# A gated mix of a state-space convolution and a spectral filter on one core: new instruction sequences with 64 fewer spare matmuls, one scale folded into its neighbours, six output rows on two other engines

## The chip, the cores and the metric

The kernel runs as one program on one NeuronCore of a Trainium2 chip. The metric is the device time of an execution in microseconds (us). The names of the engines in the profile: PE is TensorE (matmuls; PEld is its weight load), DVE is VectorE, ACT is ScalarE, POOL is GpSimd, and SP is SyncE, which here only starts DMA transfers.

## What is computed

The output is a mix of two branches over an input of 2048 positions by 640 channels. Branch a convolves each channel with a kernel K that is made from the parameters; branch b is a two-dimensional real Fourier transform, a product with complex weights, and the inverse. The gate g is one number for each position.

```python
def _A_ref(u, log_A_real, A_imag, C_real, C_imag, log_dt, D_skip):
    dt = jnp.exp(log_dt)
    A = -jnp.exp(log_A_real) + 1j * A_imag
    C = (C_real + 1j * C_imag) * dt[:, None]
    P = jnp.exp((A * dt[:, None])[:, :, None] * pos[None, None, :])
    K = 2.0 * jnp.einsum("dn,dnl->dl", C, P).real
    Kf, Uf = jnp.fft.rfft(K, L2), jnp.fft.rfft(u_t, L2)
    y = jnp.fft.irfft(Uf * Kf[None, :, :], L2)[:, :, :L]
    return y + u * D_skip[None, None, :]
def _B_ref(x, w_r, w_i):
    X = jnp.fft.rfft2(x, axes=axes) * (w_r + 1j * w_i)
    return jnp.fft.irfft2(X, s=(S, D), axes=axes)
x = A_u
g = _sigmoid((x * gate_w).sum(-1, keepdims=True))
return g * a + (1 - g) * b
```

## The kernel before

All Fourier transforms are matmuls with tables of cosines and sines, in two steps (64 by 64 positions). The program has five stages, which overlap at their edges.

Stage A (`phase_a`, first half) transforms the input: `stage1w` (L532) and `stage2` (L546) are PE matmuls, ACT (later DVE too) copies each result out of PSUM (L579), and SP writes it to the DRAM buffer `u_d` (L626). At the same time `phase_p` works out the parameters from C, A and dt on DVE, with a few ACT functions: magnitude and angle of C (an arctangent at L489, finished by L490 to L498) and a logarithm (L511). They are split into bfloat16 parts and sent through DRAM.

Stage F (second half of `phase_a`) is branch b in nine blocks: transposes (L700), products along the channels (L710), the filter on DVE (L728 to L746), and the way back (L764, then L771 and L773 on DVE).

Stage B (`phase_b`) makes K in 40 steps. For each step PE multiplies the parameters with a table of positions; ACT then takes exponentials for the magnitudes (`mags`, L832 on PE, L833 on ACT) and sines for the phases (`outer` and `inner`, L840 on PE, L846 and L852 on ACT); DVE (L860 to L862) and POOL (L865, L866) multiply magnitude and phase; PE sums over the states (`kgen`, L876), and ACT copies the sums out (L882). Stages F and B share the time between about 80 and 380 us: their instructions are interleaved on every engine. The exponential and the sine lie in different function tables of ACT, so that each change from one to the other loads a table (ACT_TABLE_LOAD).

Stages C and D transform K, multiply it with the transformed input in `fronts` (L971 to L974), transform back in `backs` (L988, L990, written to DRAM at L997 and L1000), and make the output rows in `last_e` (L1030, L1037) and `last_c` (L1030, then L1048 for the last quarter of the channels, L1050 and L1051 for the others). The output of the last quarter is written in three chunks of 6, 6 and 4 rows of 160 numbers for each partition; a row is one instruction of L1048.

Nothing is scheduled at run time. The functions only record their operations in a list; the table `ORDER` is a permutation of that list, and `Program.write` issues the operations in that order. Each engine runs its own operations strictly in that order, and an operation waits until what it reads is written and the buffer that it writes is free. Two kinds of operations do no part of the computation, and `ORDER` places them as well. `SPARE` gives a number of matmuls of a constant with itself (L406), 128 by 128, whose result nobody reads; there are 278. `PRIME` gives a number of one-element ACT functions (L409), placed ahead of the first use of another function table, so that the load happens there; there are 23 for the exponential, 23 for the sine, and one each for arctangent, logarithm and sigmoid.

Of the kernel before, what the change touches and what calls it, by code (L numbers as in the profile page):

```python
# [412 lines left out]
def phase_p(tc, A, T):  # L413
# [3 lines left out]
    with ExitStack() as ctx:  # L417
# [72 lines left out]
        V.tensor_scalar(out=ph[:, :, :], in0=ph[:, :, :], scalar1=1.0 / (2 * math.pi), scalar2=None, op0=ALU.mult)  # L490
        V.tensor_scalar(out=y[:, :, :], in0=ph[:, :, :], scalar1=-2.0, scalar2=0.25, op0=ALU.mult, op1=ALU.add)
        V.tensor_tensor(out=y[:, :, :], in0=y[:, :, :], in1=ab[:, :, :], op=ALU.mult)
        V.tensor_tensor(out=ph[:, :, :], in0=ph[:, :, :], in1=y[:, :, :], op=ALU.add)
# [449 lines left out]
def phase_d(tc, A, T, ctx, out):  # L943
# [95 lines left out]
    def last_c(c, a, n):  # L1039

        oe = oes.pop((c, a))
        p = last("p_c", lambda g: T.e3[c < 3], lambda g, r: t3s[c][r, 4 * a + n * g:4 * a + n * g + n], n)
        ot = o2.tile([128, 2, 3, 160], F32, tag="ot", name="ot")
        if c == 3:
            for j in range(2):
                for i in range(n):
                    x = 8 * j + a + i
                    V.scalar_tensor_tensor(out=ot[:, j, i], in0=p[:, j, i], scalar=T.gate[:, 0, x:x + 1], in1=oe[:, j, i], op0=ALU.mult, op1=ALU.add)  # L1048
        else:
            V.tensor_tensor(out=ot[:, :, 0:n], in0=p, in1=gate(0, a, n), op=ALU.mult)  # L1050
            G.tensor_tensor(out=ot[:, :, 0:n], in0=ot[:, :, 0:n], in1=oe[:, :, 0:n], op=ALU.add)  # L1051
        (G if c < 2 else nc.sync).dma_start(out[c].rearrange("p (j a) d -> p j a d", j=2)[:, :, a:a + n], ot[:, :, 0:n])
# [24 lines left out]
SPARE = (128, 278), (32, 0)  # L1077
PRIME = 23, 23, 1, 1, 1
# [97 lines left out]
```

## Time and profile before

| what | us |
|---|---|
| median of 3 runs | 536.0 |
| the three runs | 535.62, 536.0, 543.41 |
| the profiled execution, whole time | 533.92 |
| its span in the profile | 531.9 |

The profile is one execution of the program. Its page gives the busy time of each engine and groups of instructions by source line; a row of a group reads line, engine, operation, output and inputs, count, then busy us and mean ns, then the idle time of the engine just ahead of these instructions. The share of slices in which the engines are busy shows the stages: ACT and DVE are nearly full in the middle and ACT is nearly idle in stage D, where the DMA engines are full instead.

```profile
PE   8999999899999989999989999998999997999993
DVE  5994236989899999598688696879575673767754
ACT  3787887699989877899969989966433242332210
DMA  8969526782313335132040231413997799799986
```

Each digit is the busy share in a fortieth of the span, in tenths. PE looks full everywhere, but in the middle a part of its work is the spare matmuls.

### The profile page before, as it was taken

Reading aid. Unit: us, or ns where it says so; the run is one execution under the profiler, and the core shown is the slowest. Engines: PE = TensorE matmul, PEld = TensorE weight load, DVE = VectorE, ACT = ScalarE, POOL = GpSimd, SP = SyncE. Lnnn points to the kernel's source line nnn. Section 1 sums busy time; section 2 is a strip of 40 time slices with the busy share of each in tenths; the row PEclk is TensorE's granted clock in tenths of the full one; section 3 lists DMA queues with packets and bytes.
Section 4 is the critical chain, followed back from the end, with each engine's and each line's share of the span. In section 5 each row is a group of like instructions: output and inputs, shape, how many; then the busy total and the mean of one; then the engine's idle time right before and its main releaser. Section 6 shows DMA issues by size and latency. Waiting matters only on the chain. (4 is left out here: it accounts for less than half of the span.)

```text
span 531.9 us, 19458 instructions
## 1 busy us (share of the span) xinstructions
PE 499.3 (94%) x8600; PEld 409.5 (77%) x8600; DVE 397.6 (75%) x548; ACT 354.6 (67%) x505; POOL 226.1 (43%) x236
## 2 busy tenths in 40 slices
PE   8999999899999989999989999998999997999993
PEld 6899797788887878877768888886797886887740
DVE  5994236989899999598688696879575673767754
ACT  3787887699989877899969989966433242332210
POOL 1003213674766253746554525526431245337350
PEclk9999999999999999999989999999999999999998
DMA  8969526782313335132040231413997799799986
GB/s 318 361 199 339 171 81 215 250 256 84 101 67 110 125 103 170 46 118 70 30 147 32 67 110 52 127 55 123 358 338 240 247 374 390 261 321 311 340 266 234
DMA packets 58363, 101.17 MB, mean 190 GB/s; under 512 B 4980, under 2 KB 42136, under 8 KB 58248
## 3 DMA queue, kind: packets, MB, share of 16 engines
q1 hardware_dynamic: 34680, 67.82, 37.2%
q10 hardware_dynamic: 20368, 21.79, 12.3%
q0 software_dynamic: 3232, 10.33, 5.8%
q8 instruction: 67, 1.10, 0.8%
q14 instruction: 16, 0.13, 0.1%
HBM read 60.60 MB, written 39.65 MB: 188 GB/s over the span
## 5 line engine op out<-in xcount | busy, mean ns | idle before, releaser
L546 PE MATMUL psum<-sbuf,sbuf 128*64 128x160 f32 x1056 | 89.2, 308 | 6.5 <-ACT sbuf L536 2.7
L546 PEld LDWEIGHTS psum<-sbuf,sbuf 128*64 128x64 f32 x1056 | 72.7, 134 | 19.3 <-issue 6.5
L406 PE MATMUL psum<-sbuf 128*128 128x128 f32 x556 | 79.0, 287 | 0.0
L532 PE MATMUL psum<-sbuf,sbuf 128*64 128x128 f32 x1280 | 77.2, 274 | 0.2 <-issue 0.2
L406 PEld LDWEIGHTS psum<-sbuf 128*128 128x128 f32 x556 | 67.0, 192 | 11.3 <-issue 9.1
L532 PEld LDWEIGHTS psum<-sbuf,sbuf 128*64 128x64 f32 x1280 | 72.2, 137 | 3.8 <-issue 2.5
L710 PE MATMUL psum<-sbuf 64*128 64x161 f32 (+1 forms) x864 | 68.9, 305 | 4.3 <-DVE sbuf L771 2.2
L710 PEld LDWEIGHTS psum<-sbuf 64*128 64x128 f32 (+1 forms) x864 | 60.8, 182 | 9.4 <-DVE sbuf L771 2.3
L862 DVE TENSOR_TENSOR sbuf<-sbuf,psum 128x1024 f32<-128x1024 f32 x40 | 48.5, 1216 | 25.3 <-ACT psum L852 25.2
L833 ACT ACTIVATE sbuf<-psum 128x1024 f32<-128x1024 f32 (+1 forms) x80 | 60.9, 803 | 4.8 <-PE psum L832 3.1
L409 ACT ACT_TABLE_LOAD x48 | 61.6, 1283 | 0.8
L974 POOL TENSOR_TENSOR sbuf<-sbuf 128x320 f32<-128x320 f32 (+1 forms) x36 | 32.1, 893 | 68.3 <-DVE sbuf L972 57.3
L990 ACT COPY sbuf<-psum 128x640 f32<-128x640 f32 x32 | 21.9, 693 | 52.3 <-PE psum L988 36.1
L865 POOL TENSOR_TENSOR sbuf<-sbuf,sbuf 128x512 f32<-128x512 f32 x24 | 34.0, 1417 | 31.2 <-ACT sbuf L846 22.4
L579 ACT COPY sbuf<-psum 128x512 f32<-128x512 f32 (+2 forms) x58 | 35.3, 626 | 17.1 <-PE psum L532 11.7
L536 ACT COPY sbuf<-psum 128x512 f32<-128x512 f32 x40 | 23.9, 620 | 34.2 <-PE psum L532 22.8
L852 ACT ACTIVATE psum<-psum 128x1024 f32<-128x1024 f32 x40 | 40.3, 1008 | 9.3 <-PE psum L840 9.2
L876 PEld LDWEIGHTS psum<-sbuf 128*32 128x32 f32 x2560 | 37.9, 110 | 9.1 <-issue 7.1
L876 PE MATMUL psum<-sbuf 128*32 128x64 f32 x2560 | 44.4, 221 | 0.5 <-issue 0.4
L988 PEld LDWEIGHTS psum<-sbuf,sbuf 64*128 64x128 f32 x528 | 37.6, 186 | 6.8 <-issue 4.6
L988 PE MATMUL psum<-sbuf,sbuf 64*128 64x160 f32 x528 | 42.7, 305 | 0.1
L846 ACT ACTIVATE sbuf<-psum 128x1024 f32<-128x1024 f32 x40 | 40.7, 1017 | 2.8 <-PE psum L840 2.8
(133 smaller groups left out, 827.9 us busy)
## 6 DMA issues: line engine op xcount, KB each, us to landing
u_d<-sbuf SPq DMA_DIRECT2D x32, 320.0 KB, 4.2
sbuf<-u_d ACTq DMA_DIRECT2D x16, 640.0 KB, 6.7
s_d<-sbuf ACTq DMA_DIRECT2D x24, 320.0 KB, 5.8
sbuf<-s_d SPq DMA_DIRECT2D x6, 960.0 KB, 8.4
sbuf<-in_w_l SPq DMA_DIRECT2D x8, 644.0 KB, 4.1
sbuf<-u_d SPq DMA_DIRECT2D x8, 640.0 KB, 4.8
k_d<-sbuf SPq DMA_DIRECT2D x20, 256.0 KB, 2.3
sbuf<-k_d SPq DMA_DIRECT2D x8, 640.0 KB, 6.9
```

What stands on the lines that cost most here:

```text
L406: nc.tensor.matmul(spare[x:x + cols, i, :], c1[:, x:x + cols], c1[:, 128:256], start=True, stop=True)
L409: nc.scalar.activation(prime[0:1, i:i + 1], c1[0:1, 0:1], f)
L532: nc.tensor.matmul(p[64 * ri:64 * ri + 64, q // 4, 0:512].rearrange("p (h x) -> p h x", h=2)[:, :, 64 * (q % 4):64 * (q % 4) + 64], src[:, ...
L546: nc.tensor.matmul(p[64 * j:64 * j + 64, y, 160 * ro:160 * ro + 160], T.w2[:, x, ro, :], t1[:, x // 2 if x < 32 else K0 // 2, :, x % 2 if ...
L579: return (V.tensor_copy if T.dve and dst.home.name == "ut" else S.copy)(dst, src)
L710: P.matmul(p[:st.nl, c, 161 * i:161 * i + 161], src[r, k, x, 0:st.nl], td[r, w, k, :], start=k == 0, stop=k == 2)
L833: S.activation(ef[:, :, c:c + n], p[:, :, 0:n], AF.Exp)
L846: S.activation(sc.rearrange("p d v i -> p (d v i)"), p.rearrange("p j w -> p (j w)"), AF.Sin, scale=TWO_PI)
L852: S.activation(f, f, AF.Sin, scale=TWO_PI)
L862: V.tensor_tensor(out=x[:, 0].rearrange("p d (h j) -> p d h j", h=2), in0=e[:, :, 0:64].rearrange("p d (h j) -> p d h j", h=2), in1=cx.uns ...
L876: P.matmul(st.pb[32 * r:32 * r + 32, o, :], y[:, ri, 4 * qq + r, :], x[:, ri, 4 * qq + r, :], start=t % 2 + qq + 1 - ri == 0, stop=t % 2 * ...
L988: P.matmul(p[:, j, 160 * i:160 * i + 160], T.w3[r, pr, im, :], t2[r, h + i, im], start=im == 0, stop=im == 1)
```

## The change

Three things change.

First, in `phase_p` the arctangent's factor 1/(2 pi) no longer has an instruction of its own. The line that multiplied `ph` is gone; the next line takes -1/pi in place of -2, and the addition after it becomes a `scalar_tensor_tensor` that multiplies and adds at once.

Second, in `last_c`, for the last quarter of the channels, the first two rows of the second half of each chunk, so six rows of 16, are no longer one DVE instruction each. ACT multiplies the row with the gate out of PSUM, and POOL adds the row of the other branch.

Third, `ORDER` is another permutation, and its fillers change in number: `SPARE` from 278 to 214, `PRIME` from 23 and 23 to 25 and 24.

```diff
         S.activation(ph[:, :, :], q[:, :, :], AF.Arctan)
-        V.tensor_scalar(out=ph[:, :, :], in0=ph[:, :, :], scalar1=1.0 / (2 * math.pi), scalar2=None, op0=ALU.mult)
-        V.tensor_scalar(out=y[:, :, :], in0=ph[:, :, :], scalar1=-2.0, scalar2=0.25, op0=ALU.mult, op1=ALU.add)
+        V.tensor_scalar(out=y[:, :, :], in0=ph[:, :, :], scalar1=-1.0 / math.pi, scalar2=0.25, op0=ALU.mult, op1=ALU.add)
         V.tensor_tensor(out=y[:, :, :], in0=y[:, :, :], in1=ab[:, :, :], op=ALU.mult)
-        V.tensor_tensor(out=ph[:, :, :], in0=ph[:, :, :], in1=y[:, :, :], op=ALU.add)
+        V.scalar_tensor_tensor(out=ph[:, :, :], in0=ph[:, :, :], scalar=1.0 / (2 * math.pi), in1=y[:, :, :], op0=ALU.mult, op1=ALU.add)
...
                     x = 8 * j + a + i
-                    V.scalar_tensor_tensor(out=ot[:, j, i], in0=p[:, j, i], scalar=T.gate[:, 0, x:x + 1], in1=oe[:, j, i], op0=ALU.mult, op1=ALU.add)
+                    if j and i < 2:
+                        S.activation(ot[:, j, i], p[:, j, i], AF.Copy, scale=T.gate[:, 0, x:x + 1])
+                        G.tensor_tensor(out=ot[:, j, i], in0=ot[:, j, i], in1=oe[:, j, i], op=ALU.add)
+                    else:
+                        V.scalar_tensor_tensor(out=ot[:, j, i], in0=p[:, j, i], scalar=T.gate[:, 0, x:x + 1], in1=oe[:, j, i], op0=ALU.mult, op1=ALU.add)
...
-SPARE = (128, 278), (32, 0)
-PRIME = 23, 23, 1, 1, 1
+SPARE = (128, 214), (32, 0)
+PRIME = 25, 24, 1, 1, 1
...
-2 0 2190 2167 3 7 1 2191 4+2 8 6 2192 9 2169 19 2170 2172+3 2168 2184 2175 20+16 2176 12 2177+5 36 2182+2 2185 17 2187 10 2171 38+16 37 11 54 2186 55
...
```

What the new order does is best seen in the rows of an engine. A row names the line, the operation, what it writes and reads (a number at the end is a memory area), its shape, and how many alike follow each other. Line numbers after L490 are lower by one in the changed kernel, and from L1050 on higher by three.

The first place is PE in the middle of the program, ahead of the longest run of spare matmuls. L832 are the matmuls of `mags`, L406 the spare ones, L700 transposes. Before:

```order
L832 LDWEIGHTS sbuf_68
L832 MATMUL psum_77<-sbuf_68 128x256
L406 MATMUL psum_77<-sbuf_67 128x128 x19
L832 LDWEIGHTS sbuf_68
L832 MATMUL psum_77<-sbuf_68 128x512
L832 LDWEIGHTS sbuf_68
L832 MATMUL psum_77<-sbuf_68 128x512
```

And in the changed kernel, at the same `mags`:

```order
L831 LDWEIGHTS sbuf_68
L831 MATMUL psum_77<-sbuf_68 128x256
L406 MATMUL psum_77<-sbuf_67 128x128 x13
L831 LDWEIGHTS sbuf_68
L831 MATMUL psum_77<-sbuf_68 128x512
L831 LDWEIGHTS sbuf_68
L831 MATMUL psum_77<-sbuf_68 128x512
```

The run of 19 has become one of 13; at this point 46 spare matmuls have been issued before and 31 now.

The second place is PE at the forward products (L710) of a later block, which stand at about 250 us in the profile of before. L876 is `kgen`, L700 the transposes. Before:

```order
L406 MATMUL psum_77<-sbuf_67 128x128 x6
L710 MATMUL psum_77<-sbuf_73 128x161 x12
L832 LDWEIGHTS sbuf_68
L832 MATMUL psum_77<-sbuf_68 128x512
L832 LDWEIGHTS sbuf_68
L832 MATMUL psum_77<-sbuf_68 128x512
L406 MATMUL psum_77<-sbuf_67 128x128 x5
L876 MATMUL psum_77<-sbuf_71 32x64 x32
```

And now:

```order
L406 MATMUL psum_77<-sbuf_67 128x128 x2
L709 MATMUL psum_77<-sbuf_73 128x161 x12
L699 MATMUL psum_77<-sbuf_67,sbuf_73 128x64 x16
L406 MATMUL psum_77<-sbuf_67 128x128 x3
L839 LDWEIGHTS sbuf_69
L839 MATMUL psum_77<-sbuf_68,sbuf_69 128x256
```

The transposes, which stood one `kgen` later, have come ahead of it, the pair of `mags` has gone to another place, and 5 spare matmuls stand where 11 stood.

The third place is the end of ACT's program. Before, its last work is the copies and writes of `backs`:

```order
L990 COPY sbuf_69<-psum_77 128x2x2x160
L997 DMA s3f_d<-sbuf_72 32x160
L1000 DMA s3f_d<-sbuf_69 64x4x160 x2
L997 DMA s3f_d<-sbuf_72 32x160
L1172 UNCONDITIONAL_BRANCH
```

And now:

```order
L989 COPY sbuf_69<-psum_77 128x2x2x160
L996 DMA s3f_d<-sbuf_72 32x160
L999 DMA s3f_d<-sbuf_69 64x4x160 x2
L1048 ACTIVATE sbuf_73<-psum_77,sbuf_67 128x160 x6
L1175 UNCONDITIONAL_BRANCH
```

The six rows of `last_c` stand behind everything that ACT did before; POOL's six additions (L1049) likewise come last on POOL.

143 rows, old and new, of the table ORDER are left out of this document.

## The prediction

> **What bounds the kernel now.** I read the page first, then the busy time by stage, then who waits for whom, then the order of time around the spare matmuls, and last the end of the program. The page and the stage in which F and B overlap:
>
> ```profile
> PE 499.3 (94%) x8600; PEld 409.5 (77%) x8600; DVE 397.6 (75%) x548; ACT 354.6 (67%) x505; POOL 226.1 (43%) x236
> L406 PE MATMUL psum<-sbuf 128*128 128x128 f32 x556 | 79.0, 287 | 0.0
> 80.00:380.00 300.00, 286.41 (x5334) 234.65 (x5332) 254.02 (x320) 254.44 (x341) 156.81 (x152) 0.99 0.37 117
> ACT psum L852 <- PE psum L840: 9.2, 8, 3.4
> ACT sbuf L753 <- PE psum L710: 7.3, 9, 1.5
> DVE sbuf L862 <- ACT psum L852: 16.7, 10, 5.6
> PE psum L710 <- DVE sbuf L771: 2.2, 1, 2.2
> ```
>
> The second row is the spares: 278 operations (two passes each, so 556 records) fill 79.0 us of PE. The third row is the stretch from 80 to 380 us: after its length come the busy times of PE, weight load, DVE, ACT and POOL, then the granted clock and the share of the DMA engines. PE is busy for 286.4 of 300 us, but without the 79.0 it has 207 us of real work, and DVE and ACT have 254 each. So in the middle no engine is full with useful work: ACT and DVE each stand idle for about 46 us, waiting in turn for PE and for each other, and PE's own waits are covered by spares. Of PE's uncovered waits the longest is the 2.2 us of the last row.
>
> Are the spares themselves on the path? That shows where a run of them ends:
>
> ```profile
> 119.71 0.50 PE L832 MATMUL psum<-sbuf 48*128 48x512 bf16 x4
> 120.14 4.51 PE L406 MATMUL psum<-sbuf 128*128 128x128 f32 x38
> 122.18 1.28 ACT L409 ACT_TABLE_LOAD   x1
> 123.58 3.05 ACT L833 ACTIVATE sbuf<-psum 128x1024 f32<-128x1024 f32 x4
> 124.63 0.76 PE L832 MATMUL psum<-sbuf 48*128 48x512 bf16 x4
> 125.32 0.94 PE L406 MATMUL psum<-sbuf 128*128 128x128 f32 x6
> ...
> 257.76 2.72 PE L406 MATMUL psum<-sbuf 128*128 128x128 f32 x22
> 259.41 1.00 ACT L846 ACTIVATE sbuf<-psum 128x1024 f32<-128x1024 f32 x1
> 260.46 0.96 PE L840 MATMUL psum<-sbuf,sbuf 64*128 64x256 bf16 x8
> ```
>
> At 120.14 PE begins 19 spares (38 records). The next `mags` matmul needs a PSUM buffer that ACT frees with the first of four exponentials; these start at 123.58 and take 1.00 us for a buffer, so the buffer is free at 124.6, and PE goes on at 124.63. At 257.76 it is the sine of L846, which ends at 260.41, and PE goes on at 260.46. A run of spares thus stands in for a wait of PE on ACT and ends when the wait ends, within 0.1 us here. The middle is bounded by the chain ACT to PE to ACT (and DVE), not by PE.
>
> After 380 us the bound is another:
>
> ```profile
> 380.00:400.00 20.00, 19.41 (x308) 18.65 (x306) 14.41 (x22) 7.40 (x12) 7.97 (x11) 1.00 0.97 364
> 480.00:496.00 16.00, 15.91 (x222) 12.54 (x200) 12.44 (x18) 4.11 (x7) 9.51 (x10) 1.00 1.00 326
> sum 116.00, PE 111.82 PEld 94.08 DVE 76.36 ACT 37.78 POOL 46.13; mean PE 18.64 PEld 15.68 DVE 12.73 ACT 6.30 POOL 7.69
> ...
> 0.00:40.00 40.00, 37.28 (x698) 32.01 (x700) 33.43 (x60) 26.82 (x48) 3.13 (x9) 1.00 0.79 292
> 40.00:80.00 40.00, 38.53 (x642) 34.84 (x641) 14.19 (x26) 31.85 (x52) 10.00 (x17) 1.00 0.57 197
> ```
>
> These are the first and last of six stretches from 380 to 496 us and their sum: PE is full with real work (111.8 of 116 us), and the DMA engines nearly so (0.97 and 1.00 here). The last two rows are stage A, where PE has real work for 75.8 of 80 us.
>
> **The change part by part.**
>
> *Spares.* Two runs of the rows above give the price: 38 records take 4.51 us and 6 take 0.94, so 16 spares more take 3.57 us, 0.223 us each, with 0.27 us for a run whatever its length. In PE's listing of before there are 63 runs with 278 spares: 62.0 + 17.0 = 79.0 us, just the page's row. The new order has 54 runs with 214: 47.7 + 14.6 = 62.3 us. So 16.7 us of filling go, most of it between the places that stood at 110 and 325 us. What is it worth? If the new order has as much less waiting for PE as it has less filling, the middle shrinks by 16.7 us. That is a reading of the order's fillers and not of a measured wait: before, the fillers fit the waits, as shown, and PE's uncovered waits are few; I take it that they fit as well after. Without runs' fixed part it would be 64 x 0.223 = 14.3 us, with the mean of the page's row (79.0 / 278) 18.2 us. If the fillers only went and the waits stayed, it is worth 0. I take 16.7, because the fit of the old fillers is the nearest evidence; both ends stay for the range.
>
> Is there room? In 283.3 us (300 - 16.7) DVE's 254 us would be 90%. ACT gets more work:
>
> *Table loads.* `PRIME` grows by three (two exponentials, one sine), and ACT's listing has three table loads more, all between 80 and 380 us.
>
> ```profile
> L409 ACT ACT_TABLE_LOAD  x48: 1283/1283/1283, 22.4 to 344.6; - x48
> L409 ACT ACTIVATE sbuf<-sbuf x49: 191/202/204, 15.6 to 345.9; 1x1 f32<-1x1 f32 x49
> ```
>
> Three loads with their one-element functions take 3 x 1.485 = 4.5 us, so ACT would have 258.9 us of work in 283.3, 91%, and its idle time would fall from 45.6 to 24.4 us. That fits, but not with much to spare. The loads' price lies inside the middle: 0 if ACT's lost idle time holds it, 4.5 us at most. I take 0, since the new fillers already stand for an order with these loads; a sum that counts them in full is 4.5 us longer.
>
> *The arctangent's scale, the start and stage D.*
>
> ```profile
> L490 DVE TENSOR_SCALAR sbuf<-sbuf x1: 489/489/489, 24.9 to 24.9; 128x640 f32<-128x640 f32 x1
> 11.17 0.33 SPq L605 DMA_DIRECT2D sbuf<-in_t_w  x1
> 12.03 0.33 SPq L586 DMA_DIRECT2D sbuf<-in_u_l  x1
> 26.29 2.93 PE L546 MATMUL psum<-sbuf,sbuf 128*64 128x160 f32 x35
> sbuf<-in_t_w SPq DMA_DIRECT2D x3, 704.0 KB, 9.0
> ```
>
> L490 goes and takes 0.49 us of DVE with it; the addition that now multiplies too stays an instruction of the same size. DVE runs this while PE does stage A's 75.8 us of real work, which covers it: 0, at most -0.5. If that cover were gone, the parameters would be ready 0.5 us sooner. On SP's queue the third part of the table `w2` (L605, at 11.17) moves behind one more load of `u` that waits for PE (at 12.03), so it leaves about a microsecond later, and with 9.0 us to land is there at about 22; the second step, L546, gets to its last third during the 2.93 us from 26.29. Cost 0, or 1 us if the queue is slower. In stage D the order of `last_e` and `last_c` among `backs` changes, but the work is the same and PE's whole idle time there is 116 - 111.8 = 4.2 us: that is the most it could gain, and I take it as the most it could lose; 0 in the sum.
>
> *Six rows on ACT and POOL.* The end of the program:
>
> ```profile
> 524.93 3.08 DVE L1048 SCALAR_TENSOR_TENSOR sbuf<-psum,sbuf,sbuf 128x160 f32<-128x160 f32 x10 [0.69 <-PE psum L1030]
> 525.89 0.77 PE L1030 MATMUL psum<-sbuf,sbuf 64*32 64x320 f32 x16 [0.99 <-issue]
> L992 ACT COPY sbuf<-psum x4: 286/286/287, 418.0 to 504.3; 64x160 f32<-64x160 f32 x4
> L974 POOL TENSOR_TENSOR sbuf<-sbuf x36: 513/876/1115, 382.5 to 507.0; 128x320 f32<-128x320 f32 x32, 64x160 f32<-64x160 f32 x4
> ```
>
> Before, DVE ends its ten rows of the last two chunks at 528.01, and the last transfer follows. After, the last chunk is ready when PE ends at 526.66. ACT's two rows, by the copy of as many elements, take 0.29 each and end at about 526.95 and 527.24. POOL's additions take 0.51 each (its shortest row is of 160 elements), one after the other: 527.5 and 528.0. DVE's two rows end near 527.3. So the last chunk leaves at 528.0 to 528.2 instead of 528.01, with POOL last where DVE was last. The first two chunks leave up to 0.5 us sooner, which the last transfer does not need. Cost 0, from -0.7 (if POOL hands over at once and the transfers no longer queue) to +0.7 (with hand-overs between engines). Nothing queues behind the ACT rows: they are ACT's last.
>
> *What is not in the order: collisions and the clock.*
>
> ```profile
> L688 DVE TENSOR_TENSOR sbuf<-sbuf x18: 541/758/3934, 92.6 to 265.9; 128x384 f32<-128x384 f32 x16, 64x384 f32<-64x384 f32 x2
> 268.70:272.10 3.40, 1.22 (x18) 1.09 (x20) 3.39 (x5) 2.50 (x4) 2.38 (x4) 1.00 0.28 77
> 272.10:275.50 3.40, 3.40 (x28) 2.78 (x25) 2.00 (x2) 0.75 (x1) 0.00 (x0) 0.50 0.87 211
> ```
>
> One L688 instruction, from 265.9, took 3.93 us where its kind takes 0.54 at best; everything on DVE behind it came late, PE waited the 2.2 us shown above, was busy for 1.22 of 3.40 us, and the next 3.4 us ran at clock 0.50. That one event cost about 2.2 + 1.7 = 3.9 us. [...] 0 in the sum.
>
> The sum against the profiled execution: 533.92 - 16.7 = 517.2. The median of the runs stands 536.0 - 533.92 = 2.1 us above it, so I forecast 519.3 us. A measurement of this kernel can tell about 2% from no change, 10.7 us: below 525.3 is faster, above 546.7 slower.
>
> **The rivals.**
>
> *Part of the gain.* ACT becomes the chain: with 258.9 us of work and waits that cannot be covered, the middle gives half, 8.3 us: 536.0 - 8.3 = 527.7. For it: ACT falls from 45.6 us of idle to 24.4, and 4.5 us of loads are new. Against: DVE and ACT still have 9% and more each.
>
> *None.* Fillers were taken out and the waits stayed. Then PE stands idle where it filled, and the time is 536.0, up to 540.5 with the loads. For it: PE waits for ACT, and fewer spares speed up nothing by themselves. Against: the runs of before end with the waits, so their lengths do follow them.
>
> *Slower, by the clock.* It takes no gain at all, and uncovered waits. PE then has 16.7 us more idle time in the same 300. By the two rows above a stretch of 3.4 us with 2.2 us idle halves the clock of the next, which costs 1.7 us of work. 16.7 us are enough for seven such stretches, 7 x 1.7 = 12 us: 548. It decides from the seventh, so all of that idle time would have to come in pieces of 2.2 us. [...]
>
> **How the numbers follow.** The forecast has 0.64 (512 to 525), more gain than that 0.05 (the event of 265.9 gone and stage D better as well), part of the gain 0.12, none 0.13, slower 0.06. The predicted time is the forecast's. The range is 512 to 536: 512 is 519.3 less the 1.5 us between 16.7 and 18.2, the 3.9 of the event and 2 of stage D's 4.2; 536 is no gain. Outside lie the 0.05, the 0.06 and half of "none", 0.18 together. Faster is 0.64 + 0.05 = 0.69, the same 0.12 + 0.13 = 0.25, slower 0.06.
>
> **What would show it.** Right: the stretch up to the last `kgen` is some 17 us shorter, spares have about 62 us of PE, ACT's idle time in the middle is near 24 us, PE's own waits stay as short as they were, and the runs of spares still end with an ACT instruction. Wrong: PE idles in the middle by ten microseconds or more, ACT's idle time stays over 40, the clock shows more than one or two stretches of 0.50. The end is right if the last POOL addition ends some 1.4 us after the last matmul. The forecast fails most simply if the new fillers were not cut to the waits.

## The result, and the profile after

| | before | after |
|---|---|---|
| median of 20 runs each, us | 536.52 (530.67 to 544.8) | 538.41 (534.29 to 541.8) |
| ratio of the times, 95% interval | | 1.006 (1.0038 to 1.0081) |
| span of the profiled execution, us | 531.9 | 536.4 |

The ratio is taken over the executions within 1.5% of the fastest of the same kernel, so it is not the ratio of the two medians, which stand 1.9 us apart. By the ratio the change cost about 3 us (0.6%), where 16.7 us were forecast to be gained. The page of the changed kernel, first the busy times, then the row of the spares, then the granted clock in fortieths of the span:

```profile
PE 489.0 (91%) x8472; PEld 399.9 (75%) x8472; DVE 402.6 (75%) x541; ACT 359.0 (67%) x517; POOL 232.0 (43%) x242
L406 PE MATMUL psum<-sbuf 128*128 128x128 f32 x428 | 62.1, 288 | 0.0
PEclk9999899999999999999999999998999999999996
```

The spares went as counted: 62.1 us of PE instead of 79.0. But PE's share of the span fell with them. Where the time went is seen from the same instructions in both traces. The columns are the ends, in us from the span's start.

| end of | before | after | difference |
|---|---|---|---|
| last matmul of stage A's first half (L532; L531 after) | 77.8 | 86.0 | +8.2 |
| first `kgen` matmul (L876; L875) | 80.8 | 89.4 | +8.6 |
| last `kgen` matmul | 379.7 | 382.5 | +2.8 |
| last `backs` matmul (L988; L987) | 510.9 | 510.8 | -0.1 |
| last matmul (L1030; L1029) | 526.7 | 528.2 | +1.5 |
| span | 531.9 | 536.4 | +4.5 |

So there are three effects: a later start (8.6 us), a middle that is shorter by 5.8 us and not by 17, and an end that is longer by 3 us after the last matmul. Stage D made up 2.9 us in this execution up to its last `backs` matmul, and 1.6 of them were lost again up to the last matmul: 8.6 - 5.8 - 2.9 + 1.6 + 3.0 = 4.5.

*The start.* PE's rows of the changed kernel in order of time, with the start, the length, and in brackets the wait ahead and what ended it:

```profile
55.73 2.78 PE L531 MATMUL psum<-sbuf,sbuf 128*64 128x128 f32 x46
63.16 0.61 PE L831 MATMUL psum<-sbuf 48*128 48x512 bf16 x2 [4.64 <-DMA sbuf<-par_d]
63.70 5.23 PE L531 MATMUL psum<-sbuf,sbuf 128*64 128x128 f32 x48
```

The stretches of 3.4 us around them, with the length, the five busy times and the granted clock:

```profile
58.40:61.81 3.41, 0.12 (x2) 0.00 (x0) 0.00 (x0) 2.07 (x3) 2.75 (x6) 1.00 0.95 288
61.81:65.22 3.41, 2.06 (x16) 1.63 (x18) 0.00 (x0) 1.02 (x1) 0.00 (x0) 0.50 0.35 82
65.22:68.64 3.42, 3.42 (x36) 3.42 (x34) 0.00 (x0) 0.60 (x1) 0.00 (x0) 0.50 0.00 0
```

The first `mags` matmul (L831) now stands ahead of the last 24 matmuls of its block of stage A, and PE waits 4.64 us there for the magnitude parameters. Before, it stood behind them and waited 1.2 us:

```profile
59.27 0.39 PE L832 MATMUL psum<-sbuf 48*128 48x512 bf16 x1
60.84 0.49 PE L832 MATMUL psum<-sbuf 48*128 48x512 bf16 x3 [1.19 <-DMA sbuf<-par_d]
```

On POOL, which issues the loads of the parameters, the issue of the magnitudes waits longer for the write of the same data. The row of before:

```profile
53.88 1.02 POOL L818 DMA_DIRECT2D sbuf<-par_d  x2 [0.48 <-DMA par_d<-sbuf]
```

The row of after:

```profile
56.48 1.03 POOL L817 DMA_DIRECT2D sbuf<-par_d  x2 [2.39 <-DMA par_d<-sbuf]
```

After the wait the clock is 0.50 for 6.8 us: 48 records that take 2.84 us at full clock (a row of another run, at the end of this document) take 5.23.

There is a second, smaller cost ahead of it. The page's rows of the first step of the transform, before and after, end with the idle time of PE ahead of these instructions and what ended it:

```profile
L532 PE MATMUL psum<-sbuf,sbuf 128*64 128x128 f32 x1280 | 77.2, 274 | 0.2 <-issue 0.2
L531 PE MATMUL psum<-sbuf,sbuf 128*64 128x128 f32 x1280 | 81.0, 281 | 1.6 <-DMA sbuf<-in_u_l 1.6
```

With the changed order PE waits 1.6 us, up to 9.4 us from the start of the span, for a part of the input `u`; before it did not. All seven profiled executions with the changed start have this wait (1.6 to 2.7 us).

*The middle*, from the first to the last `kgen` matmul, in before:

```profile
80.80:379.70 298.90, 285.31 (x5322) 233.79 (x5312) 253.51 (x319) 253.46 (x339) 156.81 (x152) 0.99 0.37 117
```

And in after:

```profile
89.40:382.50 293.10, 272.15 (x5182) 220.31 (x5172) 255.90 (x318) 255.90 (x345) 160.53 (x154) 0.99 0.38 120
```

PE is busy for 13.2 us less and the stretch is 5.8 us shorter, so PE's idle time grows from 13.6 to 21.0 us. ACT is idle for 37.2 us instead of 45.4, not for 24.4.

*The end.* The last line of the program, where the engines meet: a row gives line, queue, instruction, count, shortest, median and longest duration in ns, and the first and last start. In before:

```profile
L1172 POOLq DRAIN  x3: 46/102/9637, 512.7 to 531.6; - x3
L1172 SPq DRAIN  x3: 7/7/13, 531.1 to 531.4; - x3
```

And in after:

```profile
L1175 POOLq DRAIN  x3: 46/102/6643, 529.0 to 536.2; - x3
L1175 SPq DRAIN  x3: 7/7/13, 533.0 to 535.9; - x3
```

SP's first DRAIN comes when the last output has landed, at 531.1 before and at 533.0 after: the last write of the output was issued at 528.0 and 529.8 and took 3.0 and 3.1 us to land. POOL's long DRAIN began at 512.7 before and was over at 522.3, long before that; after, it begins at 529.0 (POOL's last addition ends at 529.76) and ends at 535.6, 2.6 us after the last output. In all 18 traces the span ends 0.8 us after the later of the two.

### The profile page after: what moved, and what is told of

Its sections match the earlier page's. It is cut to its first block, busy times and chain, and to the rows that moved or that the text cites. A ratio compares the mean times of both kernels' runs of the same rounds, so it can differ in the third digit from the quotient of the medians.

```text
span 536.4 us, 19217 instructions
## 1 busy us (share of the span) xinstructions
PE 489.0 (91%) x8472; PEld 399.9 (75%) x8472; DVE 402.6 (75%) x541; ACT 359.0 (67%) x517; POOL 232.0 (43%) x242
## 5 line engine op out<-in xcount | busy, mean ns | idle before, releaser
L545 PEld LDWEIGHTS psum<-sbuf,sbuf 128*64 128x64 f32 x1056 | 72.9, 134 | 15.4 <-issue 9.1
L531 PE MATMUL psum<-sbuf,sbuf 128*64 128x128 f32 x1280 | 81.0, 281 | 1.6 <-DMA sbuf<-in_u_l 1.6
L531 PEld LDWEIGHTS psum<-sbuf,sbuf 128*64 128x64 f32 x1280 | 75.7, 141 | 5.1 <-issue 2.4
L832 ACT ACTIVATE sbuf<-psum 128x1024 f32<-128x1024 f32 (+1 forms) x80 | 60.8, 800 | 9.1 <-PE psum L831 7.1
L406 PE MATMUL psum<-sbuf 128*128 128x128 f32 x428 | 62.1, 288 | 0.0
L406 PEld LDWEIGHTS psum<-sbuf 128*128 128x128 f32 x428 | 51.8, 191 | 9.9 <-issue 8.2
L865 POOL TENSOR_TENSOR sbuf<-sbuf,sbuf 128x512 f32<-128x512 f32 x24 | 34.8, 1450 | 37.0 <-ACT sbuf L845 30.4
L875 PE MATMUL psum<-sbuf 128*32 128x64 f32 x2560 | 46.1, 225 | 2.4 <-ACT sbuf L832 1.2
L875 PEld LDWEIGHTS psum<-sbuf 128*32 128x32 f32 x2560 | 39.3, 113 | 11.1 <-issue 7.0
L987 PEld LDWEIGHTS psum<-sbuf,sbuf 64*128 64x128 f32 x528 | 37.6, 186 | 8.0 <-issue 5.8
L987 PE MATMUL psum<-sbuf,sbuf 64*128 64x160 f32 x528 | 42.7, 305 | 0.7 <-DVE sbuf L1053 0.2
L864 POOL TENSOR_TENSOR sbuf<-sbuf,sbuf 128x512 f32<-128x512 f32 x24 | 33.0, 1379 | 21.4 <-ACT sbuf L845 14.3
```

What stands on the lines that cost most here:

```text
L406: nc.tensor.matmul(spare[x:x + cols, i, :], c1[:, x:x + cols], c1[:, 128:256], start=True, stop=True)
L531: nc.tensor.matmul(p[64 * ri:64 * ri + 64, q // 4, 0:512].rearrange("p (h x) -> p h x", h=2)[:, :, 64 * (q % 4):64 * (q % 4) + 64], src[:, ...
L545: nc.tensor.matmul(p[64 * j:64 * j + 64, y, 160 * ro:160 * ro + 160], T.w2[:, x, ro, :], t1[:, x // 2 if x < 32 else K0 // 2, :, x % 2 if ...
L832: S.activation(ef[:, :, c:c + n], p[:, :, 0:n], AF.Exp)
L865: G.tensor_tensor(out=y[:, 0], in0=e[:, :, 64:96], in1=sc[:, 1], op=ALU.mult)
L875: P.matmul(st.pb[32 * r:32 * r + 32, o, :], y[:, ri, 4 * qq + r, :], x[:, ri, 4 * qq + r, :], start=t % 2 + qq + 1 - ri == 0, stop=t % 2 * ...
```

## The experiments

Each kernel was timed against the kernel before on the same chip. The theories that the expectations number grew with the runs. The columns: ratio with its 95% interval, then from the profiled execution the end of the first `kgen` matmul, the time from there to the end of the last one, and from there to the end of the span, in us.

| run | ratio | first `kgen` | middle | rest |
|---|---|---|---|---|
| before | | 80.8 | 298.9 | 152.2 |
| after | 1.006 (1.0038 to 1.0081) | 89.4 | 293.1 | 153.9 |
| before_fewer | 0.9971 (0.9931 to 1.001) | 80.7 | 297.5 | 152.4 |
| after_fewer | 0.9972 (0.993 to 1.0015) | 84.9 | 291.5 | 153.8 |
| before_loads | 1.0333 (1.0268 to 1.0398) | 82.7 | 318.7 | 159.7 |
| before_dve | 1.0266 (1.0207 to 1.0325) | 80.4 | 315.4 | 153.1 |
| before_start | 1.0017 (0.9975 to 1.0059) | 84.3 | 292.9 | 157.1 |
| late_mags | 1.0 (0.996 to 1.004) | 84.1 | 293.3 | 156.1 |
| start_only | 1.0043 (1.0004 to 1.0083) | 81.9 | 301.4 | 149.8 |
| before_end | 0.9955 (0.9913 to 0.9996) | 88.4 | 293.1 | 152.2 |
| rows_dve | 0.9972 (0.9938 to 1.0007) | 84.9 | 292.3 | 153.4 |
| before_rows | 1.0079 (1.0036 to 1.0122) | 80.7 | 298.9 | 153.4 |
| rows_first | 0.9951 (0.9916 to 0.9987) | 80.6 | 298.8 | 150.0 |
| before_scale | 0.9941 (0.9896 to 0.9986) | 80.3 | 296.5 | 150.3 |
| after_middle | 0.9913 (0.9861 to 0.9964) | 83.2 | 295.9 | 153.2 |
| mid_scale | 0.9951 (0.9916 to 0.9986) | 87.0 | 291.9 | 154.1 |
| best_parts | 1.0 (0.9966 to 1.0035) | 83.9 | 299.5 | 150.8 |
| after_mended | 0.9932 (0.9897 to 0.9967) | 83.9 | 293.0 | 153.7 |

**Are the spares on the path?** Two kernels, before and after, each with 64 spares fewer and nothing moved:

```diff
-SPARE = (128, 278), (32, 0)
+SPARE = (128, 214), (32, 0)
```

> The kernel before with 64 spare matmuls fewer (278 to 214), every run of them shortened in proportion; nothing is moved. Theory 2 (PE isn't the bound of the middle: the spare matmuls stand in waits that last as long without them, and only 9.3 us of the 79 delay a matmul that could have run): the stretch from the first to the last kernel-spectrum matmul, 298.9 us before, becomes 295 to 299 us, PE's uncovered idle grows by 13 to 17 us, ratio 0.992 to 1.002. Rival (the prediction's step: each spare matmul is 0.223 us of the path, with 0.27 us for a run): that stretch 282 to 285 us, time 518 to 522 us, ratio 0.967 to 0.973.

> The changed kernel with 64 spare matmuls fewer again (214 to 150), every run shortened in proportion; nothing is moved. Theory 2: the stretch from the first to the last kernel-spectrum matmul, 293.1 us in the changed kernel, stays at 291 to 294 us (only 4.4 us of its filling is pure delay), unless longer idle stretches of PE lower the granted clock, which would make it 294 to 300 us; ratio 1.00 to 1.01. Rival (filling is on the path): 277 to 280 us, ratio 0.975 to 0.98.

The middle of before_fewer, in the same columns as above:

```profile
80.70:378.20 297.50, 272.22 (x5192) 220.76 (x5182) 253.04 (x318) 252.83 (x339) 156.75 (x152) 0.99 0.37 118
```

PE is busy for 13.1 us less (285.31 - 272.22) and the stretch is 1.4 us shorter: 11.7 us turned into idle time. In after_fewer PE is busy for 15.7 us less and the middle fell from 293.1 to 291.5. Theory 2 holds and the prediction's step falls: a microsecond of filling is worth about 0.1 us (1.4 of 13.1, 1.6 of 15.7), and that is less than this stretch varies between kernels that leave it alone (296.5 to 301.4, below). By the lower end of before_fewer's interval, 64 spares are worth at most 3.7 us. The feared loss by the clock did not show: the stretch's clock stayed 0.99 in both. after_fewer's ratio missed its forecast of 1.00 to 1.01; why it lies so far below the changed kernel's 1.006 stays open.

**What is on the path, then?** Two kernels add work to the kernel before, one on ACT, one on DVE:

```diff
-PRIME = 23, 23, 1, 1, 1
+PRIME = 28, 28, 1, 1, 1
```

```diff
             V.tensor_tensor(out=mm[:nl], in0=xx[:nl], in1=ww[:nl], op=ALU.mult)
+            V.tensor_tensor(out=mm[:nl], in0=xx[:nl], in1=ww[:nl], op=ALU.mult)
```

> The kernel before with ten more table loads on ScalarE, in five pairs spread over the middle (every eighth of its 42 loads is followed by a load of the other table and of its own again): 10 x 1.48 us (1.283 and the 0.202 of the small activation) = 14.9 us more ScalarE work. Theory 2 (the middle is a chain that goes between TensorE, ScalarE and VectorE, so that ScalarE's time counts in part): the stretch from the first to the last kernel-spectrum matmul, 298.9 us before, becomes 303 to 310 us, time ratio 1.008 to 1.02. Rival a (ScalarE alone is the bound): 312 to 314 us, ratio 1.025 to 1.028. Rival b (such loads hide in ScalarE's 45 us of idle time, as the prediction took for the three added): 298 to 300 us, ratio 0.998 to 1.003.

> The kernel before with the product L728 of stage A's second half issued twice (same inputs, same output): 9 x 1.6 = 14.4 us more VectorE work in the middle. Theory 2: VectorE's time counts in part, 302 to 309 us from the first to the last kernel-spectrum matmul (298.9 before), ratio 1.005 to 1.018. Rival a (VectorE alone is the bound): 312 to 313 us, ratio 1.025. Rival b (ScalarE alone is the bound, VectorE's idle time takes it): 298 to 300 us, ratio 0.998 to 1.003.

The row of the loads in before_loads:

```profile
L409 ACT ACT_TABLE_LOAD x58 | 74.4, 1283 | 1.0
```

The product and its double, which stands one line further down, in before_dve:

```profile
L729 DVE TENSOR_TENSOR sbuf<-sbuf 128x1288 f32<-128x1288 f32 (+1 forms) x9 | 17.3, 1924 | 0.3
L728 DVE TENSOR_TENSOR sbuf<-sbuf 128x1288 f32<-128x1288 f32 (+1 forms) x9 | 14.9, 1650 | 0.6
```

Ten loads more, 14.9 us of ACT's time, cost 0.0333 x 535.6 = 17.8 us (14.4 to 21.3). The doubled product took 17.3 us of DVE's time, more than the 14.4 expected, and cost 0.0266 x 535.6 = 14.2 us (11.1 to 17.4). So a microsecond more costs 1.2 us on ACT (1.0 to 1.4), and some 0.8 on DVE (0.6 to 1.0), although each of them is idle for 45 us of this stretch. Part of ACT's price may be the clock: it was 0.970 to 0.978 in the executions behind that ratio, and 0.988 in the mean in those of before. Both fell nearer to "this engine alone is the bound" than to theory 2's partial price, and both cannot be alone. That fits work that goes from one to the other in turn, where each one's idle time is the time of the other; this is concluded from the two prices and was not followed step by step. The middle of before_loads (318.7) isn't used as a price, since its clock was lower still in the profiled execution, 0.96:

```profile
82.70:401.40 318.70, 293.18 (x5322) 241.24 (x5313) 254.23 (x319) 268.82 (x359) 157.09 (x152) 0.96 0.34 110
```

**What does the start cost?** before_start is the changed kernel with the order of before up to the end of stage A's first half; start_only is the reverse. late_mags is the changed kernel with one move:

```diff
 24 matmuls L531, 20 matmuls L615
+2 matmuls L831 (the first mags)
-2 matmuls L831 (the first mags), ahead of the 24 L531
```

> The changed kernel, with the order of the kernel before (and its separate scaling instruction) up to the last matmul of stage A's first half (L532), and the changed order from there on. Theory 1 (the changed start costs 8.2 us, because the first magnitude matmul stands earlier in PE's queue than its loaded parameters allow): the middle begins about 8 us earlier, the last kernel-spectrum matmul ends near 374-376 us, and the time is 530 to 533 us, ratio 0.988 to 0.994. Rival (the rest of the program absorbs a late start anyway, stage D being bound by its transfers): 536 to 538 us, ratio 1.00 or above.

> The changed kernel with the first two magnitude matmuls (L831), their exponential and its table load moved behind the rest of stage A's first half and the 20 L615 matmuls; nothing else moves. Theory 1 (PE waits 4.64 us there for the parameters, and the clock at a half after it costs about 3 us more): PE waits under 1 us there, no row at half clock follows, the last matmul of stage A's first half ends near 78-80 us, and the time is 531 to 534 us, ratio 0.990 to 0.995. Rival (another wait of PE takes its place, for the copies or the same parameters): 537 to 539 us, ratio 1.00 to 1.005.

> The kernel before with only the changed start (up to the last matmul of stage A's first half, the scale folded); the rest in the order of before. Theory 1 (PE's wait of 3 to 4.6 us for the magnitude parameters is on the path, at times with a half clock behind it): the first kernel-spectrum matmul ends at 84 to 89 us (80.8 before), the last one at 382 to 388 us (379.7), span 535 to 540 us, ratio 1.006 to 1.015. Rival (what comes later takes the late start in): span 531 to 533 us, ratio 0.997 to 1.002.

The ratios of these three decide little: 1.0017, 1.0 and 1.0043, with intervals that all touch the changed kernel's. late_mags missed its forecast (0.990 to 0.995). The traces tell more. In late_mags PE waits 0.32 us for the parameters, no half clock follows, and the first `kgen` matmul ends at 84.1 instead of 89.4. That is still 3.3 us later than before; the wait for `u`, 2.7 us in this execution, is still there. And the same start, unchanged, showed very different waits for the parameters in five profiled executions:

| run with the changed start | wait of the first L831, us | first `kgen`, us |
|---|---|---|
| after | 4.6 | 89.4 |
| before_end | 4.1 | 88.4 |
| after_fewer | 3.0 | 84.9 |
| rows_dve | 3.0 | 84.9 |
| start_only | 0.6 | 81.9 |

The load lands at a time that differs by 4 us from run to run; late_mags and after_mended, which have the same order up to it, saw it land at 62.9 and 59.4. With waits of 4 us and more the clock halved behind them, and the start was late by 8 us; with 3.0 it was late by 4, with 0.6 by 1. So the start costs 1 to 8 us by the run. The order of before is not safe from it either: in mid_scale, which has that start with the folded scale, a wait of 1.8 us for the same parameters was followed by half clock (40 records of L615 took 1.30 us, against 0.77 in rows_dve), and its first `kgen` came at 87.0. The forecast of 530 to 533 us for before_start was a miss: its first `kgen` came at 84.3 and not at 80.8, since the joined order waits at the joint, and the rest took 157.1 us instead of 153.9. start_only's 2.3 us (0.0043 x 535.8) lie between its two theories.

**What does the end cost?** before_end is the changed kernel with before's order after the last `kgen`, and all 16 rows on DVE; rows_dve has only the rows back on DVE. before_rows and rows_first are the kernel before with all six rows, or only the first chunk's two, on ACT and POOL. The second differs from the first by:

```diff
-                    if j and i < 2:
+                    if j and i < 2 and not a:
```

> The changed kernel, with the order of the kernel before after the last kernel-spectrum matmul (stage D, queue orders of the end) and all 16 last rows on VectorE. Theory 1 (the six rows and the changed order of the outputs cost about 3 us at the end, and the 3 us that stage D made up were its slack taking in the late start): 535 to 536 us, ratio 0.997 to 0.999. Rival (stage D's changed order itself is 3 us shorter, and the end costs as much): 538 to 540 us, ratio 1.003 to 1.007.

> The changed kernel with all 16 last rows on VectorE, each of the six standing where GpSimd's addition stood; every other instruction and every queue in the changed order. Theory 3 (the end costs 4.6 us because of the order of SP's queue, where reads of the last s3f_d parts stand behind output writes, and the outputs leave late and together; the six rows themselves cost nothing): from the last L987 matmul to the span's end 24.5 to 26 us as in the changed kernel (25.6), ratio 1.004 to 1.008. Rival (the six rows' hand-over from ScalarE to GpSimd is what is late): 20.5 to 22.5 us as before (21.0), ratio 0.998 to 1.002.

> The kernel before with only the six of the last 16 rows made by ScalarE and GpSimd, each pair standing where the row's VectorE instruction stood; every other instruction and every queue as before. Theory 4 (the hand-over to GpSimd makes the last outputs late): from the last L988 matmul to the span's end 23 to 25.5 us (21.0 before), ratio 1.003 to 1.009. Rival (the prediction's step: the last addition ends 1.4 us after the last matmul and costs nothing): 20.3 to 21.7 us, ratio 0.998 to 1.002.

> The kernel before with only the first chunk's two of the six rows made by ScalarE and GpSimd; the other four stay on VectorE, nothing else moves. Theory 4b (the rows cost 2.9 us because a clearing instruction at GpSimd's end, the row DRAIN of the program's last line, ends 5.89 us after GpSimd's last addition in every run so far, 2.8 us after the last output has landed; with only the first chunk's rows it ends before that): GpSimd's last addition ends about 5 us before the last matmul, the time from the last matmul to the span's end is 5.2 to 5.7 us as before (5.2; 8.3 with all six), ratio 0.998 to 1.002. Rival (the hand-over from ScalarE to GpSimd delays the outputs): 6 to 7 us there, ratio 1.002 to 1.006.

The meeting of the engines in before_rows:

```profile
L1176 POOLq DRAIN  x3: 46/102/6643, 525.6 to 532.7; - x3
L1176 SPq DRAIN  x3: 7/7/7, 529.3 to 532.5; - x3
```

And in rows_first:

```profile
L1176 POOLq DRAIN  x3: 46/102/6452, 521.5 to 529.1; - x3
L1176 SPq DRAIN  x3: 7/7/7, 528.6 to 528.9; - x3
```

With all six rows the outputs have landed at 529.3, but POOL's DRAIN lasts from 525.6 to 532.2 and the program ends behind it; the time after the last matmul is 8.3 us instead of 5.2. With two rows that DRAIN is over at 527.9, before the outputs at 528.6, and the time after the last matmul is 5.1 us. Theory 4b holds and the hand-over costs nothing: two rows were handed over as well, at no cost. The six rows alone cost 0.79% (0.36 to 1.22), and 2.9 us in the trace. rows_dve, without them, is at 0.9972 where the changed kernel is at 1.006, but after_fewer, which keeps them, is at 0.9972 too, so that pair alone shows no price. Theory 3, that SP's order was to blame, falls with rows_dve's trace: it keeps that order, and its time from the last `backs` matmul to the end fell from 25.6 to 20.4 us. (In the two profiled executions stage D took most of that back, 133.0 against 128.3 us, as it varies.) before_end, at 0.9955, has an interval that holds the forecast of its theory 1 and not that of its rival.

**The middle and the scale alone, and joins.** after_middle is before with only the middle in the new order, before_scale has only the folded scale, mid_scale both. best_parts joins before's order up to the first 64 `kgen` matmuls, the changed order up to the last `backs` matmul, and before's end. after_mended is late_mags with all rows on DVE.

> The kernel before, with only the stretch from the last matmul of stage A's first half to the last kernel-spectrum matmul in the changed order (64 spare matmuls fewer, three table loads more); start, stage D and the 16 last rows as before. Theory 1 (the middle became 5.4 us shorter and not 16.7): 530 to 532.5 us, ratio 0.988 to 0.993. Rival a (the middle saves the full filling once it starts on time): 520 to 524 us, ratio 0.97 to 0.977. Rival b (stage D takes back what the middle saves): 535 to 537 us, ratio 1.0.

> The kernel before with only the scale of the arctangent folded into the two other instructions (one VectorE instruction of the parameters less); nothing is moved. All theories: no stretch changes by more than 0.7 us, ratio 0.997 to 1.002. A rival, that the parameter chain sets when the parameters are loaded and so when the first magnitude matmul can run: that matmul ends 0.3 to 0.7 us earlier than 59.7 us.

> The kernel before with the changed middle and with the scale folded; start, stage D and the 16 rows as before. If the two ratios measured alone (0.991 and 0.994) are both real and add: 526 to 530 us, ratio 0.982 to 0.990. Rival (the 0.994 of the scale alone was the scatter of the runs, since its head ends only 0.4 us earlier): 531 to 534 us, ratio 0.990 to 0.996.

> A join of the parts that were shorter: the order of the kernel before up to the first 64 kernel-spectrum matmuls, the changed order from there to the last L987 matmul, the order of the kernel before for the rest, all 16 rows on VectorE, the separate scaling instruction kept; 225 spare matmuls. If the stretches measured add up (start 80.8, first to last kernel-spectrum matmul 293 to 295, stage D 128.3, end 21): span 523 to 525 us, time 525 to 528 us, ratio 0.978 to 0.985. Rival (a stretch that begins earlier meets transfers that do not): span 528 to 532 us, ratio 0.99 to 1.00.

> The changed kernel with its two costs undone: the first two magnitude matmuls behind the rest of stage A's first half, and all 16 last rows on VectorE. Theory (start 84.1, first to last kernel-spectrum matmul 293, from there to the end 152.5 to 153.5): span 529.5 to 531 us, time 531.5 to 534 us, ratio 0.990 to 0.996. Rival (the costs overlap with others, and the gain of the middle is all taken in by stage D): ratio 0.997 to 1.002.

The middle in the new order took 291.5 to 295.9 us in the nine profiled executions that have it whole, against 296.5 to 301.4 in the six with the order of before and nothing added. The medians, 293.1 and 298.8, are 5.8 us apart, and 4.4 us of it stand beside the cut of the spares (297.5 in before_fewer less 293.1 in after). That after_middle gave 0.9913 agrees with theory 1. before_scale's 0.9941 was not expected; its first `kgen` came only 0.5 us earlier, and mid_scale did not add it to after_middle's gain. Whether that ratio is more than scatter stays open. rows_first, whose two rows cost nothing, came out at 0.9951 (0.9916 to 0.9987) as well: a ratio 0.6% below 1 does not by itself show a shorter path here, and after_middle's is not far from it. best_parts was a miss: 81.8 us from the first `kgen` matmul to the 320th, where both parents take 75 to 76, so a joint in the middle of an order costs what the parts would bring. after_mended came out as its theory had it, at 0.9932 (0.9897 to 0.9967), clear of the changed kernel's 1.006. Its traced middle is 5.8 us shorter than that of before and its end is mended; its first `kgen` is still 3 us late, and the span is 1.3 us shorter than that of before (530.6 and 531.9). That it is faster than before by more than such scatter is not shown.

## Why the prediction was wrong

*Spares, -16.7.* This is the step that failed: "If the new order has as much less waiting for PE as it has less filling, the middle shrinks by 16.7 us". The count was right (62.3 forecast, 62.1 measured), the price was not: 64 spares fewer gave 1.4 us in before_fewer and 1.6 in after_fewer, and the rest turned into idle time of PE. The rows that were read for it said so already. They showed each run of spares ending within 0.1 us of an ACT instruction, and a filler that ends with the wait does not make the wait: without it PE stands idle until the same moment. The rows argue for the end that was put at 0, and the step took them as evidence for the other end. The rest of the middle's 5.8 us is the new order of the work itself; which of its moves brings it wasn't tried.

*Table loads, 0.* The step said that ACT's 45.6 us of idle time would hold them. In before_loads idle time of 45.4 us did not hold ten more: each cost 1.4 to 2.1 us (14.4 to 21.3 over ten), clock included. By that three cost 4.3 to 6.4 us, an estimate that was not run by itself; if it holds, the new order pays for them out of what it saves elsewhere. ACT's idle time in the middle fell to 37.2 us and not to 24.4, because the stretch did not shrink as forecast.

*Start, 0 to 1.* The third part of `w2`, on which the cost was put, does not show. What shows was left out: the place of the first `mags` matmul in PE's queue, and POOL's loads that feed it. Ahead of that, PE waits for a part of `u` (1.6 to 2.7 us), which the step did not have either; what in the new order makes that wait wasn't tried. Cost together 1 to 8 us, by the run.

*Stage D, 0 with 4.2 either way.* From the last `kgen` to the last `backs` matmul 131.2 before and 128.3 after, but 129.2 to 133.0 in other executions of the new order: inside the bound, and not a steady gain.

*Six rows, 0.* The place was right, the last addition on POOL ended 1.6 us after the last matmul (1.4 forecast). Its price was not: 2.6 us in after and 2.9 in before_rows, through the DRAIN behind it, which the sum did not have.

*Collisions and clock, 0 in the sum and 3.9 in the range.* No run shows that the L688 instruction of 265.9 was a collision, or what made it take 3.93 us; in the profiled execution of the changed kernel the longest DVE instruction of that line (L687) took 1.40 us. In size the 3.9 was about right: the half clock of the start cost at most 3.4 us (half of 6.8), but it came behind a wait for a DMA (4.64 us) and not behind a long instruction on DVE. In the middle, the one stretch at clock 0.50 of before (at 272.1) became two of 3.4 us (at 280.3 and 369.0), behind waits of 2.0 and 1.6 us for DVE.

*The rivals.* "None" came true, 536 to 540.5 for a measured 538.4, with the sentence that spoke for it: fewer spares speed up nothing by themselves. It had 0.13. That its number fits is luck in part: the middle did gain 5.8 us, and the start and the end, which it does not speak of, took that back. "Slower, by the clock" did not come: 21 us of idle time in the middle left the mean clock there at 0.99.

## What to carry to other kernels

Work that is placed in a wait is nearly free, and so taking it out gains next to nothing (0.1 us for a microsecond here): before a filler is priced, look at what ends it, and if that is another engine's instruction, price the other engine. Where two engines work in turn, the idle time of each may be no slack; adding work to one instruction of each shows their prices in two runs (1.2 us on ACT and 0.8 on DVE for a microsecond here). And look at an order's ends: the first instruction that waits for a load (4.64 us here), and the last instruction of each engine with what the program does behind it (POOL's DRAIN, over 5.89 us after POOL's last addition here).

## What the hardware showed that was not expected

POOL's DRAIN at the end of the program ends 5.89 us after POOL's last addition, within 0.01 us in all 18 traces, whether that addition comes 6.7 us before the end of the span or 15.5 (after: 529.76 and 535.65; before: 516.41 and 522.30). PE, ACT and DVE had DRAINs of at most 3.0 us there. Work that POOL ends less than 5.9 us before the last output lands thus lengthens the program: by 2.2 to 2.9 us in the five traces with all six rows, where it ended 2.9 to 3.7 us before, and not in rows_first, where it ended 6.6 us before.

The length of a wait alone does not tell in these traces whether the clock halves. The half-clock stretch behind the wait at the start lasted 6.83 us in after, those in the middle of before and after 3.41 us each. A wait of 2.97 us in rows_dve had no half clock behind it (the granted clock was 1.00 from 61.81 to 65.22):

```profile
61.28 0.39 PE L831 MATMUL psum<-sbuf 48*128 48x512 bf16 x2 [2.97 <-DMA sbuf<-par_d]
61.60 2.84 PE L531 MATMUL psum<-sbuf,sbuf 128*64 128x128 f32 x48
```

In best_parts a wait of 2.27 us had one, and 16 records of the second step took 2.29 us where they take 1.36 a little later:

```profile
62.39 0.50 PE L832 MATMUL psum<-sbuf 48*128 48x512 bf16 x3 [2.27 <-DMA sbuf<-par_d]
62.82 2.29 PE L546 MATMUL psum<-sbuf,sbuf 128*64 128x160 f32 x16
...
66.63 1.36 PE L546 MATMUL psum<-sbuf,sbuf 128*64 128x160 f32 x16
```

What decides between the two, no run here shows.

So one and the same start can be some 4 us longer in one execution than in another (89.4 against 84.9 for the first `kgen` in the table of five), and a few microseconds of this kernel can't be told from one profile.
